# Normalisation roots made by VectorE's Newton step instead of ScalarE, and four w2 loads with a later due time

## The chip, the cores and the metric

The kernel runs on one core of a Trainium2 chip. The metric is the device time of one launch in microseconds; the time before is a median of three runs. A second, profiled execution of the same kernel gives the trace that is read here.

## The reference

One token block of 2048 rows and 1024 columns goes through two sublayers, each behind a modulated layer norm:

```
sa, ca, ga, sb, cb, gb = six rows of silu(c) @ w_mod
h = layernorm(x) * (1 + ca) + sa
x = x + ga * (Cr @ (h @ Dr.T) - Ci @ (h @ Di.T))     # real part of a 2-D DFT
h = layernorm(x) * (1 + cb) + sb
x = x + gb * (gelu(layernorm(h) @ w1 + b1) @ w2 + b2)  # 1024 -> 3584 -> 1024
layernorm(x) = (x - mean) / sqrt(var + 1e-5)
```

So the second half needs two layer norms per row, one on x and one on h, each with its own root.

## The kernel before, in words

All of it happens in the function `fast`. It first normalises the rows (`ln1`, four groups of four row tiles), folds them by the symmetries of the DFT and multiplies by the DFT matrices (`hid_unit`, then `seq_tile` for 16 row tiles, products P and Q, lines 3046 and 3058). The 16 tiles are taken in 8 blocks of two, b = 0 to 7. For each block `ln2` makes both later norms: the sums of squares on ScalarE (line 3120), the scalings on VectorE (lines 3138 to 3162), the final scaling on ScalarE (line 3171). TensorE then transposes the rows (`turn`, line 3181), ScalarE copies them out (line 3185), and `z_tasks` makes seven combinations of them in halves of 16 bits (lines 3211, 3220, 3233), which are written to DRAM for the second half of the rows (line 3226). From about 312 us on the MLP begins: products with w1 (`product3`, line 3628), bias and GELU, products with w2 (line 3742) and the sum over 14 pairs of feature tiles. The matrices are split in seven combinations too (a fast matrix product with seven instead of eight blocks), by the helper lines 2379 (high half, ScalarE), 2391 (low half, VectorE) and 2405 (sums, VectorE).

Each root is made in two steps. `roots` (line 2619) writes on ScalarE r = sqrt(scale * v + bias) (line 2620) and the guarded variance ve = scale * v + bias (line 2621). `newton` (line 2623) improves it on VectorE in four small instructions, lines 2626 to 2629: a = 1 / r, a = a * ve, a = a + r, r = 1 / a. `ln1` calls it on 128x4 values, four times, `ln2` on 128x2 values, twice per block (`root`, lines 3128, 3160 and 3168), which makes 20.

The order of the instructions on each engine is fixed when the program is built. A planner in the kernel keeps a clock per engine and a list of tasks per stream; `pick_first` looks at the first task of every stream in the order of their due times and takes for each engine the first one that can start now, or else the one that starts earliest. A load is a task of the engine "dma" and is issued by SP (SyncE), whose queue is in order: a transfer that waits holds all behind it. Loads share eight semaphores in turn, so a load also waits until the eighth before it has landed.

The loads that matter for the change are issued between 299 and 346 us:

- `early2` (line 3494): four loads of 512 KB, rows of w2 that only serve the squares of its norm (`norm_tasks`, line 3311), which give the scale s2 of the first pair of w2's combinations (`w2_norm`). Due 240, once the products P and Q of tile 15 are done. They go to a place of their own, 144 to 160 KB.
- `raw1` (line 3491): four loads of 256 KB, raw w1 for the groups 3 and 4. Same condition, due 250, to 136 to 144 KB, where operands of product P of the last tiles have lain. Behind them in the same stream stand the four loads `raw2` of w2 (line 3497), due 240, which wait for `turn` 13.
- `w1` (lines 3480 and 3487): the split w1 of the groups 0 to 2, 256 KB each, read back from DRAM, due 200 and 255; they wait for certain turns, the row product of line 2900 or the first products with w1.
- the last block's x (line 3101, 1 MB, due 70), the row of w_mod (line 2894), and the stores of x (line 3148), which are put on SP's queue as soon as the planner has the sum that they store.

Of the kernel before, what the change touches and what calls it, by code (L numbers as in the profile page):

```python
# [12 lines left out]
AF = mybir.ActivationFunctionType  # L13
ALU = mybir.AluOpType
# [3 lines left out]
P = 128  # L18
S = 2048
D = 1024  # L20
# [5 lines left out]
EPS = 1e-5  # L26
# [5 lines left out]
SZ = 256.0  # L32
# [1959 lines left out]
def fast(ctx, tc, x, cre, cim, dre, dim, w1, b1, w2, b2, c, wm, out):  # L1992
# [3 lines left out]
    pe, act, dve, gp, sp = nc.tensor, nc.scalar, nc.vector, nc.gpsimd, nc.sync  # L1996
# [8 lines left out]
    def mk(shape, dt, tag, bufs=1):  # L2005
        cnt[0] += 1
        return pool.tile(shape, dt, tag=tag, name=f"{tag}_{cnt[0]}", bufs=bufs)
# [439 lines left out]
    def add(stream, eng, cost, fn, deps=(), key=None, due=0.0, tag=None):  # L2447
        t = Task(eng, cost, fn, deps, key)
        push(stream, tag or stream, [t], due)
        return t.key  # L2450
# [15 lines left out]
    one, eps4, epsz = (mk([P, 1], F32, n) for n in ("one", "eps4", "epsz"))  # L2466
# [22 lines left out]
    def load(name, f, deps=(), cost=1.4, stream="ld", due=0.0):  # L2489
        return add(stream, "dma", cost, f, deps, name, due)  # L2490
# [125 lines left out]
        nunit[0] += 1  # L2616
        return (nunit[0] - 1) % 3

    def roots(ve, r, v, scale, bias):
        act.activation(r, v, AF.Sqrt, scale=scale, bias=bias[:, 0:1])  # L2620
        act.activation(ve, v, AF.Identity, scale=scale, bias=bias[:, 0:1])

    def newton(ve, r, a):

        return [
            ("dve", 0.17, lambda: dve.reciprocal(a, r)),
            ("dve", 0.17, lambda: dve.tensor_tensor(a, a, ve, op=ALU.mult)),
            ("dve", 0.17, lambda: dve.tensor_tensor(a, a, r, op=ALU.add)),
            ("dve", 0.17, lambda: dve.reciprocal(r, a)),
        ]  # L2630

# [3 lines left out]
    def ln1(bt):  # L2635
        mv, lc = csum[:, 8 * bt : 8 * bt + 8].rearrange("p (q k) -> p q k", k=2), lncs[bt % 2]
        ve, r, a, nm = (lc[:, n] for n in range(4))
        cls, hb = divmod(bt, 2)
        due = 2.0 + 6.0 * bt
        for q in range(4):  # L2640
# [21 lines left out]
            k = add(f"lnq{bt}", "act", 1.35, spread, [("sum", i)], ("spread", i), due)  # L2662
        scale = 0.25 if bt < ACT_STATS else 0.25 / D
        s = [
            ("act", 0.4, lambda: roots(ve, r, mv[:, :, 1], scale, eps4)),
            *newton(ve, r, a),
            ("dve", 0.17, lambda: dve.scalar_tensor_tensor(nm, mv[:, :, 0], -1.0, r, op0=ALU.mult, op1=ALU.mult)),
        ]
        for eng, cost, f in s:
# [183 lines left out]
    for cls in range(2):  # L2853
        f = lambda cls=cls: gp.memset(FA(SPB[cls], (1, 1026), pn=64), 0.0)
# [228 lines left out]
    for n in range(2):  # L3083
        f = lambda n=n: gp.memset(FA(QS[n] + 256, (1, 1)), 0.0)
# [19 lines left out]
    def ln2(b):  # L3104
        y, w, cl = yb(b), wb(b), lns[b % 3]
        su, nm, v, ve, r, a = (cl[:, n, :] for n in range(6))
        due = 78.0 + 22.0 * b
        S_ = f"ln{b % 3}"
        last = [None]

        def step(eng, cost, f, deps=(), key=None):
            last[0] = add(S_, eng, cost, f, [last[0], *deps], key, due)
            return last[0]

        def sq(src, junk, scale, bias, free=None):
            def square(n):
                def f():
                    if free is not None:
                        free(n)
                    act.activation(  # L3120
                        junk[:, n], src[:, n], AF.Square, scale=scale, bias=bias[:, n : n + 1], accum_out=v[:, n : n + 1]
                    )

                return f

            return square

        def root(scale, bias, key=None):
            step("act", 0.4, lambda: roots(ve, r, v, scale, bias), key=key)
            for t in newton(ve, r, a):  # L3130
                step(*t)

        x1 = []
        wfree = w_free(b)
        for n in range(2):
            i = 2 * b + n
            if b in ADDED:
                step("dve", 1.23, lambda n=n: dve.tensor_tensor(y[:, n], y[:, n], ga_t, op=ALU.mult), [("y", i), ("xw", b), *rows])
                k = step("dve", 1.32, lambda n=n: dve.scalar_tensor_tensor(
                    y[:, n], y[:, n], 1.0, w[:, n], op0=ALU.mult, op1=ALU.add, accum_out=su[:, n : n + 1]))  # L3140
            else:
                last[0] = None
                k = step("dve", 1.32, lambda n=n: dve.scalar_tensor_tensor(
                    y[:, n], y[:, n], 1.0, ga_t, op0=ALU.mult, op1=ALU.mult, accum_out=su[:, n : n + 1]), [("y", i), *rows])
                store("xa", i, lambda n=n, i=i: gp.dma_start(y[:, n], x_s[i // 8, i % 8], accum_op=ALU.add), k)
                k = "st", "xa", i
            x1.append(k)
            store("x1", i, lambda n=n, i=i: sp.dma_start(o_s[i // 8, i % 8], y[:, n]), k)
        if b in ADDED:
            step("dve", 0.17, lambda: dve.tensor_scalar(nm, su, -1.0 / D, None, op0=ALU.mult))  # L3150
        else:
            step("dve", 0.17, lambda: dve.scalar_tensor_tensor(
                nm, su, -1.0 / D, csum[:, 4 * b : 4 * b + 4 : 2], op0=ALU.mult, op1=ALU.subtract))
        q = sq(y, w, 1.0, nm)
        for n in range(2):
            step("act", 1.35, q(n), [x1[n], *wfree])
        for n in range(2):
            step("dve", 1.28, lambda n=n: dve.scalar_tensor_tensor(
                w[:, n], y[:, n], nm[:, n : n + 1], cb_t, op0=ALU.add, op1=ALU.mult), key=("sw", 2 * b + n))
        root(0.25 / D, eps4)  # L3160
        for n in range(2):
            step("dve", 1.28, lambda n=n: dve.scalar_tensor_tensor(  # L3162
                w[:, n], w[:, n], r[:, n : n + 1], sb_t, op0=ALU.mult, op1=ALU.add, accum_out=su[:, n : n + 1]))

        q = sq(w, y, -float(D), su, lambda n: reuse("x1", 2 * b + n))
        for n in range(2):
            step("act", 1.35, q(n), key=("ysq", 2 * b + n))
        root(0.25 / (SZ * SZ * D**3), epsz, ("root", b))
        step("dve", 0.17, lambda: dve.scalar_tensor_tensor(nm, su, -1.0 / D, r, op0=ALU.mult, op1=ALU.mult))
        for n in range(2):  # L3170
            f = lambda n=n: act.activation(w[:, n], w[:, n], AF.Identity, scale=r[:, n : n + 1], bias=nm[:, n : n + 1])
            step("act", 1.25, f, key=("w", 2 * b + n))
# [317 lines left out]
    for g, n in ((3, 2), (3, 3), (4, 0), (4, 1)):  # L3490
        f = lambda g=g, n=n: sp.dma_start(raw1(g, n), w1[g, :, PLACE.index(n), :])
        load(("raw1", g, n), f, [("P", 15), ("Q", 15)], 0.75, "rw2", 250.0)
    for q in range(4):
        f = lambda q=q: sp.dma_start(early2(q), w2[0:2, :, q, :].rearrange("j p x -> p j x"))
        load(("early2", q), f, [("P", 15), ("Q", 15)], 1.5, "rw3", 240.0)
    for q in range(4):
        f = lambda q=q: sp.dma_start(raw2(0, q), w2[0:2, :, q, :].rearrange("j p x -> p j x"))
        load(("raw2", 0, q), f, [("turn", 13)], 1.5, "rw2", 240.0)
# [360 lines left out]
    due, t = {}, 0.0  # L3859
# [100 lines left out]
    t = clk["pe"]  # L3960
# [20 lines left out]
    for kind, k in seq:  # L3981
# [17 lines left out]
        else:  # L3999
            v = k  # L4000
# [71 lines left out]
```

## Time and profile before

| what | value |
|---|---|
| median of three runs | 1378.37 us (1377.45 to 1378.69) |
| the profiled execution's own time | 1377.23 us |
| its span | 1375.4 us, mean granted TensorE clock 0.972 |
| PE (TensorE matmul) busy | 1291.3 us, 94% |
| DVE (VectorE) busy | 1088.4 us, 79% |
| ACT (ScalarE) busy | 746.6 us, 54% |
| POOL (GpSimd) busy | 265.1 us, 19% |
| chain that ended last | PE 67%, DVE 9%, ACT 4% of the span |

The span runs from the first to the last instruction of the core. A row of a timeline gives start, duration, engine, line, operation, operands with their shapes, and in brackets how long the engine had been idle before and which instruction let it go on. "SPq" is SP issuing a transfer, not the transfer itself. PEld is TensorE's loading of weights. Line numbers are those of the kernel before.

### The profile page before, as it was taken

To read this page: it belongs to the slowest core of one execution; us is meant where nothing else is said; L and a number is where in the kernel's file an instruction comes from. 1 tells how busy PE (TensorE), PEld (TensorE's weight loads), DVE (VectorE), ACT (ScalarE), POOL (GpSimd) and SP (SyncE) were. 2 spreads that over 40 slices of the span, in tenths; PEclk is the share of its full clock that TensorE was granted. 3 is DMA by queue.
4 is the path that set the end of the run, shared out by engine and by line. 5 is a ranking of instruction groups with operands and counts; after the bars stand their busy time and mean duration, and the time that the engine had idled before them with its cause. 6 is when DMAs were issued, how large, how long until landed. Compare 5 with 4: busy or idle time off the path is not lost.

```text
span 1375.4 us, 17329 instructions
## 1 busy us (share of the span) xinstructions
PE 1291.3 (94%) x6081; PEld 622.9 (45%) x6081; DVE 1088.4 (79%) x1623; ACT 746.6 (54%) x1188; POOL 265.1 (19%) x426
## 2 busy tenths in 40 slices
PE   5888899777989999999999999999999999999997
PEld 1445466543434444444444444444444444444443
DVE  5888789998588999898989996566685858687695
ACT  4476557877667747474746433256545353636330
POOL 2000010102102000000000000254553433553201
PEclk9888899998999999999999999999999999999999
DMA  9777046569536957575453555999797878786524
GB/s 368 307 250 231 1 169 169 133 194 381 218 145 200 320 146 226 171 204 187 153 184 130 200 205 223 262 349 338 252 318 240 296 264 294 268 306 235 176 81 111
DMA packets 109754, 306.22 MB, mean 223 GB/s; under 512 B 14076, under 2 KB 14076, under 8 KB 107736
## 3 DMA queue, kind: packets, MB, share of 16 engines
q1 hardware_dynamic: 76776, 197.73, 40.5%
q0 software_dynamic: 32880, 107.29, 25.9%
q8 instruction: 49, 0.80, 0.2%
q14 instruction: 49, 0.40, 0.1%
HBM read 220.03 MB, written 84.93 MB: 222 GB/s over the span
## 4 chain that ended last, share of the span: by engine, by line
PE 67%; DVE 9%; ACT 4%; issue 2%; DMA 2%; SPq 0%; POOL 0%; DVEq 0%; ACTq 0%; POOLq 0%
PE ps L3742 34%; PE ps L3628 32%; ACT arena L2379 1%; DVE arena L2391 1%; DVE arena L3220 1%; DVE arena L2405 1%; DVE arena L3162 1%; PE ps L3046 1%; DVE arena L3233 1%; DMA arena<-fw 1%; DMA fzc<-arena 1%; ACT arena L3211 1%; DVE arena L3792 0%; DMA arena<-in_w_dram 0%; PE ps L3058 0%
## 5 line engine op out<-in xcount | busy, mean ns | idle before, releaser
L3628 PE MATMUL ps<-arena 128*128 128x512 f16 x2352 | 515.5, 381 | 9.4 <-DMA arena<-fw 4.8
L3742 PE MATMUL ps<-arena 128*128 128x512 f16 x2352 | 513.2, 380 | 8.0 <-ACT arena L3782 6.2
L3628 PEld LDWEIGHTS <-arena 128*128 128x128 f16 x2352 | 230.8, 98 | 289.9 <-issue 10.8
L3742 PEld LDWEIGHTS <-arena 128*128 128x128 f16 x2352 | 230.7, 98 | 288.3 <-issue 12.0
L3792 DVE SCALAR_TENSOR_TENSOR arena<-ps,i4c,arena 128x1024 f32<-128x1024 f32 x179 | 229.5, 1282 | 104.9 <-PE ps L3742 100.4
L2379 ACT ACTIVATE arena<-arena,shc 128x512 f16<-128x512 f32 (+1 forms) x115 | 115.8, 1017 | 137.2 <-DVE arena L2405 80.3
L2391 DVE SCALAR_TENSOR_TENSOR arena<-arena,shc 128x512 f16<-128x512 f32 (+1 forms) x115 | 129.0, 1121 | 29.6 <-ACT arena L2379 29.2
L2405 DVE TENSOR_TENSOR arena<-arena 128x512 f32<-128x512 f32 (+1 forms) x196 | 148.5, 764 | 3.7
L3533 ACT ACTIVATE arena<-arena 128x512 f32<-128x512 f32 (+5 forms) x148 | 91.2, 617 | 108.8 <-DVE arena L3542 84.8
L3647 ACT ACTIVATE arena<-arena,b1s,i1c 128x512 f32<-128x512 f32 x78 | 63.4, 813 | 90.0 <-DVE arena L3654 88.1
L2379 ACT ACTIVATE arena<-arena,s1c 128x512 f16<-128x512 f32 (+1 forms) x70 | 60.9, 886 | 66.5 <-DVE arena L2405 42.2
L3654 DVE TENSOR_TENSOR arena<-arena,ps 128x512 f32<-128x512 f32 x78 | 53.4, 685 | 52.4 <-PE ps L3628 51.7
L3542 DVE TENSOR_TENSOR arena<-arena 128x256 f32<-128x256 f32 x240 | 87.9, 421 | 1.7 <-DMA arena<-in_cre_dram 1.7
L3323 POOL PARTITION_ALL_REDUCE sums<-sums x21 | 10.4, 501 | 405.0 <-DVE sums L3319 405.0
L3559 POOL DMA_DIRECT2D arena<-in_cim_dram x99 | 54.5, 551 | 92.3 <-ACT arena L3533 86.1
L2391 DVE SCALAR_TENSOR_TENSOR arena<-arena,s1c 128x512 f16<-128x512 f32 (+1 forms) x70 | 65.8, 958 | 5.0 <-ACT arena L2379 4.9
L3559 POOL DMA_DIRECT2D arena<-in_cre_dram x99 | 54.6, 552 | 68.3 <-ACT arena L3533 50.9
L3650 ACT ACTIVATE arena<-ps 128x512 f32<-128x512 f32 x78 | 45.8, 588 | 35.8 <-PE ps L3628 35.6
L2391 DVE SCALAR_TENSOR_TENSOR arena<-arena,s2c 128x1024 f16<-128x1024 f32 x49 | 62.0, 1279 | 0.9 <-ACT arena L2379 0.9
L3046 PE MATMUL ps<-arena 128*128 128x256 f16 (+3 forms) x400 | 51.7, 290 | 10.1 <-DVE arena L3073 10.1
L2900 PE MATMUL ps<-arena,scol 128*128 128x512 f32 x128 | 58.3, 602 | 0.3 <-ACT arena L2915 0.3
L2379 ACT ACTIVATE arena<-arena,s2c 128x1024 f16<-128x1024 f32 x49 | 55.0, 1137 | 5.8 <-DVE arena L2405 5.8
(204 smaller groups left out, 1230.7 us busy)
## 6 DMA issues: line engine op xcount, KB each, us to landing
fw<-arena SPq DMA_DIRECT2D x71, 512.0 KB, 5.0
arena<-fw SPq DMA_DIRECT2D x119, 256.0 KB, 4.9
arena<-fw SPq DMA_DIRECT2D x49, 512.0 KB, 7.0
arena<-in_cre_dram POOLq DMA_DIRECT2D x96, 256.0 KB
arena<-in_cim_dram POOLq DMA_DIRECT2D x96, 256.0 KB
arena<-in_wm_dram SPq DMA_DIRECT2D x32, 512.0 KB, 7.5
arena<-in_w_dram SPq DMA_DIRECT2D x32, 512.0 KB, 6.4
arena<-in_w_dram SPq DMA_DIRECT2D x56, 256.0 KB, 4.5
```

What stands on the lines that cost most here:

```text
L2379: act.activation(o[m][0], q(j), AF.Copy, **sc)
L2391: dve.scalar_tensor_tensor(o[m][1], q(j), scale, o[m][0], op0=ALU.mult, op1=ALU.subtract)
L2405: dve.tensor_tensor(q(d), q(a), q(b), op=op)
L2900: pe.matmul(bank((6 if n < 3 else 4) + h), scol[:, k : k + 1].to_broadcast([P, P]), FA(o + 512 * h, (1, 512)), start=k == 0, stop=k == 7,)
L3046: pe.matmul(PA(pb + o, (1, w)), l, r, start=n == 0, stop=n == len(mm_) - 1)
L3533: f = lambda: act.activation(sq(a), sq(a), AF.Square, accum_out=csum[0:pn, n : n + 1])
L3542: dve.tensor_tensor(a[:, o::2], a[:, o::2], b[:, o::2], op=op)
L3559: return lambda t: gp.dma_start(t[0:pn], v)
L3628: pe.matmul(ps.rearrange("p (k t) -> p k t", k=4), w1c[:, m, s, a, d * P : (d + 1) * P], zc(m)[:, b, :, d, :], start=(start and d == 0 and ...
L3647: act.activation(dst, src, AF.Gelu_apprx_tanh, scale=inv, bias=b1s[:, 2 * p + j : 2 * p + j + 1])
L3742: pe.matmul(t[:, j], hidc[:, c_, m, a, k * P : (k + 1) * P], w2c[:, m, c_, w], start=(start and c_ == 0 and n == 0), stop=(c_ == 1 and n = ...
L3792: lambda: dve.scalar_tensor_tensor(dst, ps[b], inv, dst, op0=ALU.mult, op1=ALU.add), kp[b],
```

## The change

`roots` keeps the Sqrt on ScalarE and loses the Identity that wrote ve. `newton` gets the raw variance v, the scale and the guard, and makes the same value in its two middle steps: ve = (v + eps / scale) * a, then a = ve * scale + r. The number of VectorE instructions stays four per root; two TENSOR_TENSOR become two SCALAR_TENSOR_TENSOR with immediate scalars. The planner's cost for the ScalarE step (0.4) and for the VectorE steps (0.17) stays as it was. Besides, the due time of the four `early2` loads goes from 240 to 300.

```diff
-    def roots(ve, r, v, scale, bias):
+    def roots(r, v, scale, bias):
         act.activation(r, v, AF.Sqrt, scale=scale, bias=bias[:, 0:1])
-        act.activation(ve, v, AF.Identity, scale=scale, bias=bias[:, 0:1])
-
-    def newton(ve, r, a):
+
+    def newton(ve, r, a, v, scale, eps):
 
         return [
             ("dve", 0.17, lambda: dve.reciprocal(a, r)),
-            ("dve", 0.17, lambda: dve.tensor_tensor(a, a, ve, op=ALU.mult)),
-            ("dve", 0.17, lambda: dve.tensor_tensor(a, a, r, op=ALU.add)),
+            ("dve", 0.17, lambda: dve.scalar_tensor_tensor(ve, v, eps / scale, a, op0=ALU.add, op1=ALU.mult)),
+            ("dve", 0.17, lambda: dve.scalar_tensor_tensor(a, ve, scale, r, op0=ALU.mult, op1=ALU.add)),
             ("dve", 0.17, lambda: dve.reciprocal(r, a)),
         ]
...
-            ("act", 0.4, lambda: roots(ve, r, mv[:, :, 1], scale, eps4)),
-            *newton(ve, r, a),
+            ("act", 0.4, lambda: roots(r, mv[:, :, 1], scale, eps4)),
+            *newton(ve, r, a, mv[:, :, 1], scale, EPS / 4),
...
-        def root(scale, bias, key=None):
-            step("act", 0.4, lambda: roots(ve, r, v, scale, bias), key=key)
-            for t in newton(ve, r, a):
+        def root(scale, bias, eps, key=None):
+            step("act", 0.4, lambda: roots(r, v, scale, bias), key=key)
+            for t in newton(ve, r, a, v, scale, eps):
                 step(*t)
...
-        root(0.25 / D, eps4)
+        root(0.25 / D, eps4, EPS / 4)
...
-        root(0.25 / (SZ * SZ * D**3), epsz, ("root", b))
+        root(0.25 / (SZ * SZ * D**3), epsz, EPS / (4 * SZ * SZ), ("root", b))
...
         f = lambda q=q: sp.dma_start(early2(q), w2[0:2, :, q, :].rearrange("j p x -> p j x"))
-        load(("early2", q), f, [("P", 15), ("Q", 15)], 1.5, "rw3", 240.0)
+        load(("early2", q), f, [("P", 15), ("Q", 15)], 1.5, "rw3", 300.0)
```

## The prediction, made before the result was known

> **What bounds the kernel now.** I read first the span and clock, then the chain that ended last, then the busy time by stage.
>
> ```profile
> core 0: 1375.4 us, clock 0.972
> 476.38 36.26 PE ps L3742 x168
> ...
> 1274.09 36.26 PE ps L3742 x168
> 205.00:250.00 45.00, 37.37 (x252) 24.98 (x250) 41.05 (x79) 35.96 (x58) 4.38 (x6) 0.95 0.58 153
> 250.00:300.00 50.00, 42.95 (x276) 28.70 (x275) 46.98 (x82) 38.27 (x59) 4.29 (x5) 0.91 0.58 149
> 300.00:342.00 42.00, 30.33 (x111) 14.81 (x110) 37.66 (x65) 33.53 (x50) 11.42 (x16) 0.87 1.01 360
> 342.00:405.00 63.00, 55.88 (x258) 25.72 (x257) 45.10 (x65) 43.56 (x58) 6.21 (x9) 0.96 0.50 187
> ```
>
> The profiled execution took 1377.23 us, its span 1375.4 us, so 1.8 us lie around the span; the median of the three timed runs is 1378.37 us, 1.1 us above the profiled execution. From 476 us to 1310 us the chain is TensorE alone, one block of 168 matmuls in 36.26 us after another, so nothing that the change touches can be worth anything there. All that can be won or lost lies before 476 us. In the stage rows the columns are length, then busy time of PE, PEld, DVE, ACT and POOL, the clock, the DMA share and GB/s. Between 205 and 300 us VectorE is busy 88 of 95 us, ScalarE 74; from 300 to 342 us the DMA engines are full (1.01) and VectorE still has 37.66 of 42 us. So the second layer norm is bound by VectorE with ScalarE close behind, and its end, with the loads of w1 for the first products, by VectorE and DMA together.
>
> **The left-out ScalarE instruction.**
>
> ```profile
> L2621 ACT ACTIVATE lns<-lns,eps x8: 279/283/291, 208.9 to 346.8; 128x2 f32<-128x2 f32 x8
> L2621 ACT ACTIVATE lns<-lns,epsz x8: 279/279/280, 213.9 to 354.2; 128x2 f32<-128x2 f32 x8
> L2621 ACT ACTIVATE lnc<-csum,eps x4: 280/281/282, 12.0 to 85.4; 128x4 f32<-128x4 f32 x4
> 208.74 0.29 ACT L2620 ACTIVATE lns<-lns,eps 128x2 f32<-128x2 f32 x1
> 208.93 0.28 ACT L2621 ACTIVATE lns<-lns,eps 128x2 f32<-128x2 f32 x1
> 209.06 0.17 DVE L2626 RECIPROCAL lns<-lns 128x2 f32<-128x2 f32 x1 [0.64 <-ACT lns L2620]
> 209.33 0.16 DVE L2627 TENSOR_TENSOR lns<-lns 128x2 f32<-128x2 f32 x1
> 209.53 0.16 DVE L2628 TENSOR_TENSOR lns<-lns 128x2 f32<-128x2 f32 x1
> 209.72 0.17 DVE L2629 RECIPROCAL lns<-lns 128x2 f32<-128x2 f32 x1
> 306.17 0.16 DVE L3169 SCALAR_TENSOR_TENSOR lns<-lns 128x2 f32<-128x2 f32 x1
> L2627 DVEq EVENT_SEMAPHORE  x20: 21/21/21, 12.3 to 354.6; - x20
> ```
>
> Twenty Identity instructions go, sixteen of them in the second layer norm. Each holds ScalarE for about 0.2 us (start to start, 208.74 to 208.93), though it lasts 0.28. But the reciprocal starts behind the Sqrt, not behind the Identity: the Identity runs beside the reciprocal. So only what stands behind it on ScalarE can gain 0.2 us.
>
> VectorE keeps four instructions per root. Two TENSOR_TENSOR of 128x2 (0.16 us) become two SCALAR_TENSOR_TENSOR of 128x2, which a neighbouring line shows at 0.16 us as well: nothing for the operations. What goes is a wait: L2627 has a semaphore instruction of its own, and its start lies 0.27 us behind that of the reciprocal, where the next steps follow in 0.20 and 0.19. The new first product reads the raw sum of squares, which ScalarE wrote before the Sqrt that VectorE has already waited for, so no wait takes its place. That is 0.07 us a root at most, 0.05 where the reciprocal is the shorter one; I take 0.06.
>
> ```profile
> 209.33 0.17 DVE lns L2627
> ...
> 326.56 0.17 DVE lns L2627
> ```
>
> Of these steps 12 stand on the chain that ended last, the first at 209.33 and the last at 326.56: 12 x 0.06 = 0.7 us. The bounds are 0 (the wait stays in another form) and 12 x 0.2 = 2.4 us (ScalarE's share carried through at each); I stay at 0.7, because on the chain the roots are rows of VectorE and of the Sqrt, and the Identity isn't among them. The four roots of the first layer norm lie before the part that the chain view reaches, between 0 and 4 x 0.2 = 0.8 us; I take 0, since no view puts them on the chain.
>
> **The moved loads.** The four loads at L3494 are 512 KB each (as the code has them) and are at present first in their group on SP's queue; the four of L3491 (raw w1, 256 KB each, due 250) come behind.
>
> ```profile
> 295.04 5.30 PE L3046 MATMUL ps<-arena 128*128 128x257 f16 x24 [3.15 <-DVE arena L3073]
> 299.51 0.39 SPq L3494 DMA_DIRECT2D arena<-in_w_dram  x1
> 301.43 0.39 SPq L3101 DMA_DIRECT2D arena<-in_x_dram  x1
> 301.87 1.91 SPq L3494 DMA_DIRECT2D arena<-in_w_dram  x3
> 303.83 1.59 SPq L3491 DMA_DIRECT2D arena<-in_w_dram  x2
> 311.61 0.98 SPq L3491 DMA_DIRECT2D arena<-in_w_dram  x2
> DMA  0000996999999999999999999999999899999999
> ```
>
> With due 300 the planner takes the four L3491 loads first; then, until the turns and products that the other reloads wait for are done, its queue has nothing else ready, so I expect three L3494 loads around 302 to 305 and the fourth at 311.6, behind the store that SP holds there. By bytes: before the store four of L3494, two of L3491 and the 1 MB of L3101 went out, 3.5 MB; now three, four and that, 3.5 MB again; behind it 0.5 MB either way. The last row is the DMA share from 295 to 345 us in steps of 1.25 us: full from 303.75 on. The same bytes in the same full queue ahead of the w1 reloads cost nothing. The one new wait: the first L3491 load overwrites operands of the product at 295.04, whose end is 300.34, while the L3494 load could start at 299.51. Behind it on SP stands L3101, which goes at 301.43 either way. Price between 0 and 0.8 us; I take 0, for the byte count.
>
> The squares of these rows are four ScalarE instructions of the norm that gives w2's scale.
>
> ```profile
> L3311 ACT ACTIVATE arena<-arena x4: 1037/1052/1057, 308.6 to 322.4; 128x1024 f16<-128x1024 f32 x4
> 323.48 1.13 ACT L3120 ACTIVATE arena<-arena,lns 128x1024 f32<-128x1024 f32 x1
> 331.62 1.06 ACT L3211 ACTIVATE arena<-arena 128x1024 f16<-128x1024 f32 x1 [0.94 <-DVE arena L3233]
> 371.06 2.18 ACT L2379 ACTIVATE arena<-arena,s2c 128x1024 f16<-128x1024 f32 x2
> ```
>
> The first, now at 308.6, has no data in time and goes to the others, which end right before 323.48; the last will find its place near 331, where ScalarE waits 0.94 us. It is 1.05 us long against those 0.94, so some tenths spill over, into the 4.3 us that VectorE has idle between 300 and 342 us. The scale itself is read at 371.06, some 35 us later. I take 0 here, ends 0 and 1.2 us (one whole square in front of L3120).
>
> **What the end does with it.**
>
> ```profile
> 332.44 4.29 SPq L3480 DMA_DIRECT2D arena<-fw  x4
> 336.93 1.09 PE L3181 MATMUL ps<-ident,arena 128*128 128x128 f32 x8 [2.03 <-ACT arena L3185]
> 341.75 8.62 PE L3628 MATMUL ps<-arena 128*128 128x512 f16 x32 [3.73 <-DMA arena<-fw]
> 404.50 7.70 PE L3742 MATMUL ps<-arena 128*128 128x512 f16 x23 [6.21 <-ACT arena L3782]
> 310.76:314.18 3.42, 2.14 (x6) 0.50 1.04 404
> 341.48:344.90 3.42, 3.15 (x8) 0.50 1.03 413
> 402.92:406.34 3.42, 1.84 (x5) 0.50 0.83 334
> ```
>
> The reloads at 332.44 stand on SP behind a store that waits for VectorE, so a shorter VectorE chain moves them and with them the restart of TensorE at 341.75. The sum: 1378.37 - 0.7 + 0 + 0 = 1377.7 us (1376.5 for the profiled execution).
>
> After a pause TensorE runs at half clock (0.50 in the last three rows: length, PE busy, clock, DMA). The clock came back to full behind the stretch that was busy 3.15 of 3.42 us, not behind those with 2.14 and 1.84; so where a restart falls in such a stretch is worth up to 1.2 us: a restart 1 us earlier might spare the second half-speed stretch. The Trainium skill ("TensorE: Matmul & The Clock Gate", Part 1) says that the clock is judged in free-running windows of about 3.4 us. The trace agrees in the length, 3.42 us; by that rule an earlier restart at 341.75 stays slow until the same 344.90 and keeps only half of the 0.7, which makes 1378.0; by the row alone it keeps all, and the sum goes by that.
>
> **The rivals.** *Relief of the queue (faster).* If due 300 puts the L3494 loads behind the w1 reloads (due 200 and 255), 2.1 MB leave the full queue ahead of the load for 341.75. At 413 GB/s that is 5.1 us; TensorE's own transposes (336.93 + 1.09) end at 338.0, so 3.7 are usable, of which the half-speed stretch takes some 0.7: 1378.4 - 0.7 - 3.0 = 1374.7 us. For it: restart waits for DMA. Against: SP's queue has pauses, 305 to 311, in which loads that are ready will be sent.
>
> *Clock stretches move (faster).* If ScalarE's 0.2 us carry through at some roots, the restart in 310.76 to 314.18 comes 1 us earlier, and so does that at 404.50; both return to full clock a stretch earlier, 2 x 1.2 us, beside about 1 us of shift: 1378.4 - 3.4 = 1375.0 us. For it: 2.14 and 1.84 of 3.42 us are near the middle. Against: 0.7 us is below the 1 us that is needed.
>
> *A late restart (slower).* All four squares stand before 323.48 (+1.2), the first load waits (+0.8), and the w1 reloads slip by the 1.3 us that are left beside Newton's 0.7. Then the stretch from 341.48 is busy 1.9 of 3.42 us, as in the two rows that stayed slow, and TensorE runs at half clock 3.4 us longer: +1.7. The restart at 404.50 adds some 0.3. In all +3.3: 1381.7 us. It decides once the restart is over about 0.3 us late. For it: only 0.27 us of that stretch are free now. Against: VectorE, not ScalarE, is last before 326.
>
> *The change does nothing:* the semaphore wait stays and bytes are bytes: 1378.4 us.
>
> **How the numbers follow.** Forecast 1377.7 (0.32), nothing 1378.4 (0.02), relief 1374.7 (0.22), clock stretches 1375.0 (0.19), late restart 1381.7 (0.25). A measurement of this kernel tells about 0.2%, 2.8 us, from no change; so faster has 0.22 + 0.19 = 0.41, same 0.34, slower 0.25. The forecast's own range is 1376.0 (2.4 for the roots) to 1379.2 (0.8 for the load). With cases of both signs the range has to reach both: from 1372.8 (relief, and a clock stretch spared with its shift, 1374.7 - 1.2 - 0.7) to 1381.8 (just over the late restart); what lies outside are larger sums of the same, under 0.2.
>
> **What would show it.** L2621 has no ScalarE row, L2627 no semaphore row, and the product starts 0.20 us behind the reciprocal. In SP's rows L3491 stands before L3494, with three of the latter before 311 and one behind. TensorE restarts near 341.0, 341.75 - 0.7; a time near 338 means relief, one behind 342.0 the late restart. If the granted clock is 1.00 right behind 314.18 or 406.34, the stretches moved. I am wrong at the root if the stage from 342 to 405 us changes its length by over 1 us, since I expect its order of work unchanged.

## The result, and the profile after

The changed kernel takes 1370.15 us (median of 7 runs, 1366.74 to 1372.83) where the kernel before, beside it, takes 1377.45 us (7 runs, 1374.38 to 1378.69). The ratio is 0.9949, 95% interval 0.9932 to 0.9967: about 7 us faster, outside the range that was given. A second set of runs of the changed kernel gave 0.9951 (0.9935 to 0.9968).

First the span and clock of the kernel after, its stages, and from its chain of waits the pieces around 475 us; then the stage from 405 us of the kernel before, which had not been shown.

```profile
core 0: 1368.4 us, clock 0.973
300.00:342.00 42.00, 30.61 (x97) 14.05 (x96) 35.47 (x57) 30.83 (x45) 8.05 (x12) 0.84 0.96 350
342.00:405.00 63.00, 60.62 (x292) 28.67 (x291) 50.76 (x77) 47.79 (x61) 9.06 (x16) 1.00 0.57 208
405.00:475.00 70.00, 67.24 (x312) 30.29 (x311) 58.77 (x87) 50.62 (x66) 11.00 (x16) 1.00 0.79 223
473.10 1.21 DVE arena L3791
474.35 31.25 PE ps L3741 x144
505.61 36.26 PE ps L3627 x168
```

```profile
405.00:475.00 70.00, 68.68 (x307) 30.42 (x306) 59.51 (x90) 49.76 (x65) 11.73 (x16) 0.97 0.80 241
```

In both profiled executions the first transposes start at 217.35 us, so their times compare directly. Up to 342 us nothing is won. From 342 to 405 us TensorE is busy 60.62 us instead of 55.88 us, at clock 1.00 instead of 0.96. From 505 us on it is bound by TensorE as before, 36.26 us for 168 matmuls. So the gain is made between 342 and 475 us. The timeline of TensorE after says where:

```profile
322.47 4.26 PE L3627 MATMUL ps<-arena 128*128 128x512 f16 x12 [2.79 <-DMA arena<-fw]
341.56 2.76 PE L3627 MATMUL ps<-arena 128*128 128x512 f16 x12 [1.37 <-DMA arena<-fw]
393.29 5.34 PE L3741 MATMUL ps<-arena 128*128 128x512 f16 x24
398.92 13.32 PE L3741 MATMUL ps<-arena 128*128 128x512 f16 x61 [0.29 <-ACT arena L3781]
474.35 6.00 PE L3741 MATMUL ps<-arena 128*128 128x512 f16 x27 [2.76 <-DVE arena L3791]
```

The first two products with w2 start at 393.29 us, 0.3 us later than before (392.95). The third follows after 0.29 us of idle time instead of 6.21 us: 398.92 instead of 404.50 us. It runs at full clock, where before it crossed a half-speed stretch; by the fifth product the lead is 8.2 us, and 10.0 us at 466.25 us, two short waits of before, 0.70 and 0.62 us, being gone as well. A new wait of 2.76 us at 474.35 us takes 2.9 us back; 7.0 us remain to the end (1368.4 against 1375.4). A pause costs twice when the clock is low behind it: 6.21 us idle was followed by clock 0.50, 2.76 us idle by 1.00. The Trainium skill ("TensorE: Matmul & The Clock Gate", "Why this matters for your kernels") advises against gaps above about 3 us for that reason; these two rows agree. The length alone does not decide, though: the pause of 2.79 us ahead of 322.47 us in the same trace was followed by clock 0.50, and its 12 matmuls took 4.26 us.

The third product waits for ScalarE's copy of the first. The rows of ScalarE, before and then after:

```profile
356.94 1.23 ACT L3171 ACTIVATE arena<-arena,lns 128x1024 f32<-128x1024 f32 x1
359.02 1.23 ACT L3171 ACTIVATE arena<-arena,lns 128x1024 f32<-128x1024 f32 x1
360.25 1.28 ACT L3924 ACT_TABLE_LOAD   x1
369.12 1.13 ACT L2379 ACTIVATE arena<-arena,shc 128x1024 f16<-128x1024 f32 x1
389.13 0.72 ACT L2379 ACTIVATE arena<-arena,s1c 128x512 f16<-128x512 f32 x1 [2.39 <-DVE s1c L3340]
390.37 0.71 ACT L2379 ACTIVATE arena<-arena,s1c 128x512 f16<-128x512 f32 x1
403.36 1.09 ACT L3782 ACTIVATE arena<-ps,i4c 128x1024 f32<-128x1024 f32 x1
```

```profile
349.76 1.28 ACT L3923 ACT_TABLE_LOAD   x1
351.90 1.24 ACT L3170 ACTIVATE arena<-arena,lns 128x1024 f32<-128x1024 f32 x1
354.00 1.23 ACT L3170 ACTIVATE arena<-arena,lns 128x1024 f32<-128x1024 f32 x1
361.18 1.14 ACT L2379 ACTIVATE arena<-arena,shc 128x1024 f16<-128x1024 f32 x1
397.77 1.10 ACT L3781 ACTIVATE arena<-ps,i4c 128x1024 f32<-128x1024 f32 x1
398.76 1.33 ACT L2379 ACTIVATE arena<-arena,s1c 128x512 f16<-128x512 f32 x2
```

Two things have changed places. The first GELU, whose table load shows in the trace, stood behind the last block's two scalings (L3171) and stands ahead of them (L3170): 349.76 instead of 360.25 us, so the hidden tiles' splitting (operand shc) starts at 361.18 instead of 369.12 us. And the splitting of w1's group 3 (operand s1c) stood ahead of the copy (operand i4c) and stands behind it. Neither is in the diff. On VectorE it is one of the sums of the first products with w1 that changed places with the last block's root, here first before, then after:

```profile
348.74 0.69 DVE L3933 TENSOR_TENSOR arena<-arena,ps 128x512 f32<-128x512 f32 x1 [6.29 <-PE ps L3628]
349.35 0.16 DVE L2626 RECIPROCAL lns<-lns 128x2 f32<-128x2 f32 x1
```

```profile
344.86 0.16 DVE L2625 RECIPROCAL lns<-lns 128x2 f32<-128x2 f32 x1
349.19 0.68 DVE L3932 TENSOR_TENSOR arena<-arena,ps 128x512 f32<-128x512 f32 x1
```

The planner made these choices. Apart from the left-out Identity, the two orders first differ on ScalarE at the square of 308.65 us, on VectorE at 309.36 us and on TensorE at the transposes of 336.93 us (times of the kernel before). By the planner's rule (first in due order that can start now) a square that leaves that gap changes what fits into every later one. The runs below show that the due time alone brings the new order; that it does so by way of the squares is read from the rule and from this first difference, and no run moved the squares alone.

### The profile page after: what moved, and what is told of

Its sections match the earlier page's. It is cut to its first block, busy times and chain, and to the rows that moved or that the text cites. A ratio compares the mean times of both kernels' runs of the same rounds, so it can differ in the third digit from the quotient of the medians.

```text
span 1368.4 us, 17290 instructions
## 1 busy us (share of the span) xinstructions
PE 1290.4 (94%) x6081; PEld 624.5 (46%) x6081; DVE 1089.3 (80%) x1623; ACT 744.6 (54%) x1168; POOL 264.2 (19%) x426
## 4 chain that ended last, share of the span: by engine, by line
PE 66%; DVE 10%; ACT 3%; DMA 2%; issue 2%; POOL 0%; SPq 0%; DVEq 0%; ACTq 0%; POOLq 0%
PE ps L3741 34%; PE ps L3627 31%; DVE arena L2391 2%; DVE arena L3219 1%; DVE arena L3161 1%; ACT arena L2379 1%; DVE arena L2405 1%; PE ps L3045 1%; DMA arena<-fw 1%; DVE arena L3232 1%; PE ps L3057 1%; DVE arena L3791 1%; DMA frow_gbb<-arena 0%; DVE arena L3653 0%; DMA arena<-in_w_dram 0%
## 5 line engine op out<-in xcount | busy, mean ns | idle before, releaser
L3532 ACT ACTIVATE arena<-arena 128x512 f32<-128x512 f32 (+5 forms) x148 | 91.2, 617 | 108.5 <-DVE arena L3541 89.7
L3558 POOL DMA_DIRECT2D arena<-in_cim_dram x99 | 54.5, 550 | 92.3 <-ACT arena L3532 89.3
L3310 ACT ACTIVATE ps<-arena 128x1024 f32<-128x1024 f32 x46 | 46.7, 1016 | 19.2 <-DMA arena<-in_w_dram 9.0
```

The costliest lines, as they stand in the source:

```text
L3532: f = lambda: act.activation(sq(a), sq(a), AF.Square, accum_out=csum[0:pn, n : n + 1])
L3558: return lambda t: gp.dma_start(t[0:pn], v)
```

## The experiments

A ratio is to the kernel before on the same chip, with its 95% interval. "Copy stretch" is the time from the first to the third product with w2 in the profiled execution (before 11.55, after 5.63 us). The other columns are times behind the start of the first transposes, since that start itself lies between 212.6 and 217.7 us in different executions.

| version | median us | ratio | GELU table load | copy stretch | third w2 product | end |
|---|---|---|---|---|---|---|
| before | 1374.8 to 1377.5 | 1 | 142.9 | 11.55 | 187.2 | 1158.0 |
| after | 1370.15 | 0.9949 [0.9932, 0.9967] | 132.4 | 5.63 | 181.6 | 1151.0 |
| after, again | 1368.08 | 0.9951 [0.9935, 0.9968] | 135.0 | 5.63 | 184.5 | 1153.9 |
| new roots only | 1373.72 | 0.9987 [0.9970, 1.0004] | 142.5 | 11.56 | 186.8 | 1158.0 |
| due 300 only | 1371.96 | 0.9980 [0.9965, 0.9995] | 134.2 | 5.62 | 183.1 | 1152.7 |
| after, loads in old order | 1369.51 | 0.9965 [0.9948, 0.9981] | 134.2 | 5.64 | 183.5 | 1152.9 |
| before, loads in new order | 1376.09 | 0.9999 [0.9984, 1.0014] | 141.5 | 11.55 | 185.8 | 1156.8 |
| before, pause filled | 1373.56 | 0.9990 [0.9974, 1.0006] | 142.5 | 11.56 | 186.8 | 1157.2 |
| last norm due 205 | 1365.20 | 0.9920 [0.9902, 0.9939] | 130.4 | 5.18 | 178.6 | 1147.9 |
| after, last norm due 242 | 1366.90 | 0.9953 [0.9933, 0.9973] | 133.8 | 5.42 | 180.6 | 1151.6 |
| sum behind | 1369.87 | 0.9958 [0.9942, 0.9974] | 134.7 | 5.18 | 181.9 | 1151.1 |
| root behind | 1374.85 | 0.9993 [0.9981, 1.0005] | 144.0 | 11.12 | 188.0 | 1160.1 |
| sum moved | 1377.72 | 1.0012 [0.9997, 1.0026] | 143.0 | 11.55 | 187.3 | 1158.8 |
| sum back | 1371.66 | 0.9970 [0.9954, 0.9986] | 136.7 | 5.18 | 185.0 | 1154.6 |
| GELU behind | 1377.87 | 1.0013 [1.0001, 1.0025] | 140.1 | 11.12 | 189.2 | 1160.6 |
| GELU ahead | 1375.40 | 1.0002 [0.9991, 1.0013] | 137.9 | 6.26 | 181.8 | 1157.4 |
| w1 group 3 late | 1375.12 | 0.9995 [0.9982, 1.0008] | 140.9 | 9.21 | 182.8 | 1155.6 |
| w1 group 3, all late | 1373.30 | 0.9987 [0.9972, 1.0002] | 143.0 | 9.22 | 185.0 | 1158.8 |
| new roots, last norm due 205 | 1362.59 | 0.9912 [0.9892, 0.9932] | 130.2 | 5.18 | 177.5 | 1146.7 |

One profiled execution says less than these columns suggest. "After", "after, again", "due 300 only" and "after, loads in old order" run one and the same order of instructions on TensorE, VectorE, ScalarE and GpSimd (but for the roots' own instructions). Their copy stretch is 5.62 to 5.64 us each time, but their third product lies anywhere from 181.6 to 184.5 us and their end from 1151.0 to 1153.9 us. "Before", "new roots only" and "before, loads in new order" share the other order, with 11.55 to 11.56, 185.8 to 187.2 and 1156.8 to 1158.0 us. So the profiles bear out a gain of 3 to 7 us at the end, of which the pair shown above has the most, and a difference of under 3 us in the last two columns is not shown by one execution.

**The change in parts.** New roots with due 240, and the old roots with due 300.

> The new Newton step with the loads of w2's rows still due 240, so every engine keeps the order of work of the kernel before. If the gain is the changed order (first theory), this is worth 0 to -1 us against before, and the third product with w2 starts near 404, as before. If the ScalarE time that the left-out instruction frees is what counts (second theory), at least half of the 7 us are here and that product starts before 401.

> Only the due time goes to 300; the roots are made as before. The first theory (changed order) expects -6 to -7.5 us against before and the third product with w2 near 399, since the planner's order is that of the changed kernel. The second theory (freed ScalarE time) expects less than half of it, -3 us at most.

> The changed kernel itself, on the same chip as the next three, as their measure: 5 to 7.5 us below the kernel before.

The new roots alone keep every instruction's place: TensorE's restart (341.75 us before) comes 1.0 us earlier behind the first transposes (123.4 instead of 124.4 us), the third product with w2 0.4 us, the end 0.1 us. Due 300 alone has the changed kernel's order and its copy stretch of 5.62 us. So the order comes from the due time. By the ratios the parts are 1.8 and 2.8 us, together 4.6 us; the changed kernel with its loads in the old order gains 4.8 us on the same chip, and the changed kernel itself 6.7 us on another. The 2.8 us (interval 0.7 to 4.8) miss the 6 to 7.5 that the first theory expected; by the time alone the second theory would allow them. What speaks for the order is the copy stretch, and against freed ScalarE time that the new roots alone start the third product at 403.41 us, not before 401. No run here splits the gain more finely.

**Is it the transfers?** Both kernels once more with SP issuing the eight loads in the other's sequence, all tasks staying where they are (a table gives each load's place in the planner another load to issue).

```diff
-        load(("early2", q), f, [("P", 15), ("Q", 15)], 1.5, "rw3", 300.0)
+        load(("early2", q), issue(E_(q)), [("P", 15), ("Q", 15)], 1.5, "rw3", 300.0)
```

> The changed kernel, but its eight loads of raw w1 and of w2's rows are issued by SP in the sequence of the kernel before; the order of work on the computing engines stays that of the changed kernel. If the order of the computing engines carries the gain, the time stays within 1.5 us of the changed kernel's (1370). If the transfers' order or their share of the DMA queue carries it (third theory), 3 us or more of the 7 are lost.

> The kernel before, but SP issues its eight loads of raw w1 and w2's rows in the changed kernel's sequence; the computing engines keep the order of before, with one square of w2 early on ScalarE. First theory: no gain, 0 to +3 us, since that square now waits for its data. If the transfers' sequence carries the gain: -3 us or better.

The sequence of the transfers shows no gain by itself (0.9999, interval 0.9984 to 1.0014). Without it the changed kernel keeps 4.8 us (0.9965). Its median is within 1.5 us of 1370, as expected for the order; by the ratio it gains 2.2 us less than the changed kernel in its first runs, with intervals that overlap. So most of the gain comes with the planner's order, and not with the sequence of the transfers.

**Is it the half-speed stretch?** The kernel before with the second product issued twice, to keep TensorE busy in the pause (it then counts twice in the sum).

```diff
+                if v == 0 and blk == 0 and m == 1:
+                    part(blk, m, ps[b], (0, 1))
```

> The kernel before, with the second product with w2 (12 matmuls) issued twice, so that TensorE works some 2.6 us in its pause ahead of the third product at 404.5; all else as before, the result the same. If the half-speed stretch behind that pause is worth what the milestones show (7.76 us between the third and the fifth product before, 5.17 after), the stretch goes and the time falls by 2 to 2.6 us. If that stretch lies beside other work that is as late, the time stays within 0.7 us.

```profile
401.85 10.46 PE L3742 MATMUL ps<-arena 128*128 128x512 f16 x35 [3.62 <-ACT arena L3784]
```

0.9990, with an interval that holds 1; the 1.4 us lie between the two cases. But the run does not answer the question. The row of the third product shows that 3.62 us of the pause are left, and the first 13 matmuls behind it still run at clock 0.50 (401.85 to 407.10 us). What the half-speed stretch is worth stays open; "GELU ahead" below has no slow matmul behind its third product, and no gain.

**An earlier last norm.** My first theory was that the last block's norm (due 232) comes earlier in the changed kernel, and that this pays.

```diff
-        due = 78.0 + 22.0 * b
+        due = 78.0 + 22.0 * b if b < 7 else 205.0
```

> The kernel before, old roots, loads due 240; only the last block's norm gets due 205 instead of 232, which puts its first additions on VectorE's queue ahead of block 6's scalings, as in the changed kernel. If the gain is that this norm, and with it the splitting of w2, is done earlier, this gives 4 us or more of it, and the third product with w2 starts 4 us or more earlier than before. If the squares' or loads' new place is what counts, under 1.5 us.

> The changed kernel, new roots, loads due 300; only the last block's norm gets due 242 instead of 232. Its first additions come later (planner's order), the squares and loads stay late. First theory: 4 us or more of the gain are lost, the time is within 2.5 us of the kernel before. Rival (squares and loads): the gain stays, within 1.5 us of the changed kernel.

Due 205 in the kernel before gives 0.9920, better than the change (the intervals just overlap). But the changed kernel with due 242 keeps its gain (0.9953). An earlier norm is enough and not needed; the theory in that form falls.

**The sum at the head of VectorE's queue.** Its replacement was the 6.29 us in which VectorE waits for TensorE in front of the last block's root. Two runs change the sum's place and let the planner plan on; a third tries the splitting of w1's group 3.

```diff
# sum behind (on before); ("sb", i) is a new key of the scalings L3162
-  f, [k, ("g3e", g, n)], ("g3s", g, n), 215.0, "g3")]
+  f, [k, ("g3e", g, n), *([("sb", 15)] if (g, n) == (0, 3) else [])], ("g3s", g, n), 215.0, "g3")]
# root behind (on after)
-                step(*t)
+                step(*t, [("g3s", 0, 3)] if b == 7 and key is None else [])
# w1 group 3 late (on before): push_w1(3) moved from ahead of the loop to the end of gemm3(2)
```

> The kernel before, but VectorE's sum of the first products with w1 (L3933) may only stand behind the last block's scalings (L3162). Loads, squares, roots and all of VectorE's order up to 342 us stay those of before. Theory A (a sum at the head of VectorE's queue, waiting 6.3 us for TensorE's first products with w1 while the last block's root is ready behind it, is where the changed kernel wins): the idle 6.3 us in front of the root goes, the stretch from the first to the third product with w2 shortens from 11.55 us to 5 to 7 us, time ratio 0.993 to 0.997 (about 1369 us). Theory C (what wins is that the last block's two additions and the store behind them come 11 us earlier in the planner's order): stretch 11.5 us and ratio 0.999 to 1.001, since those stay where they are.

> The changed kernel, but the last block's first root may only stand behind VectorE's sum of the first products with w1, as it does in the kernel before. Roots, loads, squares and the early additions of the last block stay those of the changed kernel. Theory A: an idle time of 3 to 6 us is back in front of the root, the stretch from the first to the third product with w2 is 10.5 to 12 us again, ratio to before 0.998 to 1.000 (what is left is Newton's 0.7 to 1 us). Theory C: stretch 5.6 us and ratio 0.995 as in the changed kernel.

> The kernel before, but the splitting of w1's group 3 is handed to the planner only ahead of the products with w2, which puts its three VectorE pieces (1.9 us) behind ScalarE's copy of the first product. Theory B (the changed kernel wins because these pieces no longer stand ahead of that copy): stretch from the first to the third product with w2 near 5.6 us, ratio 0.995. Theory A (they only move because the idle time ahead is filled): the 6.3 us idle in front of the root stays, the stretch shortens by no more than the pieces, to 9.5 to 11.5 us, ratio 0.998 to 1.001.

In stretch and time the first two came out as theory A had it: one place in the queue gives 0.9958 on the kernel before and takes the changed kernel back to 0.9993. But the idle time that should be back in "root behind", 3 to 6 us, is only 0.66 us. The third run speaks against B, but missed A's numbers: the stretch is 9.21 us, just under A's 9.5, and the idle time in front of the sum is 0.93 us, not 6.3, at the same total time. So the wait itself could hardly be the price. Nor is the root ready for all of it, as theory A says. Rows of ScalarE before:

```profile
346.08 0.60 ACT L3928 ACTIVATE arena<-ps 128x512 f32<-128x512 f32 x1 [4.95 <-PE ps L3628]
346.58 0.29 ACT L2620 ACTIVATE lns<-lns,eps 128x2 f32<-128x2 f32 x1
```

The root's Sqrt (L2620) stands on ScalarE behind a copy that itself waits 4.95 us for TensorE, and starts only 2.8 us before the reciprocal of 349.35 us. (That place does not decide either: in "sum behind" the Sqrt still stands behind such a copy, in "root behind" ahead of it.) The next two move only that place and leave all other instructions where they are: the sum behind the scalings in the order of before, and the root behind the sum in the order of "sum behind".

```diff
# sum moved (on before): the planner's task issues nothing, the last scaling issues it
+            if (g, n) == (0, 3):
+                kept_back.append(f)
+                f = lambda: None
...
+                if (b, n) == (7, 1):
+                    kept_back.pop()()
```

> The kernel before with one single instruction elsewhere: VectorE's sum L3933 that stands ahead of the last block's root is issued behind the block's two scalings (L3162); every other instruction of every engine keeps the order of before. If the wait at the head of VectorE's queue is itself the price: the stretch from the first to the third product with w2 falls from 11.55 to 6 to 8.5 us, ratio 0.995 to 0.997. If the price is the order that the planner chooses behind it (tile 15's transposes later on TensorE, the splitting of w1's group 3 ahead of the copy): stretch 10 to 11.5 us, ratio 0.998 to 1.000.

> The earlier run that had the sum behind the scalings (ratio 0.9958), with the root's four steps and the scalings issued behind the sum again; all else keeps that run's order. If the wait itself is the price: stretch from the first to the third product with w2 9 to 11.5 us, ratio 0.998 to 1.000. If the order behind it is: stretch 5 to 6.5 us, ratio 0.995 to 0.997.

The two rows are of "sum moved": VectorE's root, and the third product on TensorE (here L3749).

```profile
347.02 0.17 DVE L2626 RECIPROCAL lns<-lns 128x2 f32<-128x2 f32 x1 [4.56 <-ACT lns L2620]
404.62 7.67 PE L3749 MATMUL ps<-arena 128*128 128x512 f16 x23 [6.21 <-ACT arena L3789]
```

The root comes 2.3 us earlier, all that the Sqrt allows, and the pause on TensorE is 6.21 us as before: 1.0012. Stretch and ratio lie just above what was expected for the order as the price, and far from theory A. With a wait put back (2.60 us in front of the sum) and the faster order kept, the stretch stays at 5.18 us and the ratio is 0.9970. Against the 0.9958 without it the wait is worth 1.7 us by the ratios, whose intervals overlap; in the two profiles the third product comes 3.0 us and the end 3.5 us later. So the wait is not what the copy stretch follows, and theory A falls as the main price, though a part of the time may be the wait's. The sum matters mainly because of the order that is planned behind it.

**GELU and w1's group 3.** All the faster versions have a table load before 137 us (in the table) and VectorE's pieces of the splitting of w1's group 3 behind the copy; none of the slower ones has both. ScalarE's two pieces need not be behind it: in "last norm due 205", "sum behind", "sum back" and "new roots, last norm due 205" they stand right ahead of the copy, and TensorE has no pause.

```diff
# GELU behind (on after)
-  f, [*deps, ("root", NB - 1)], ("quad", g, n), 266.0)
+  f, [*deps, ("root", NB - 1), *([("w", 15)] if g == 0 else [])], ("quad", g, n), 266.0)
# GELU ahead (on before)
-            step("act", 1.25, f, key=("w", 2 * b + n))
+            step("act", 1.25, f, [("quad", 0, PLACE[0])] if b == 7 else [], key=("w", 2 * b + n))
# w1 group 3, all late (on before): pushed behind the copy of the first product with w2
+                    if (v, blk, m) == (0, 0, 0):
+                        push_w1(3)
+                        push_w1(4)
```

> The changed kernel, but ScalarE's GELU of the first w1 products (with the table load before it) may only stand behind the last block's two scalings on ScalarE (L3170), as it stands in the kernel before; in the changed kernel the first GELU stands ahead of them. Roots, loads, squares, the block's additions and VectorE's sum keep their places. If this place decides: first table load 8 to 11 us later, stretch from the first to the third product with w2 10.5 to 12 us, ratio to before 0.998 to 1.000. If not: 5.6 us and 0.995.

> The kernel before, but the last block's two scalings on ScalarE (L3171) may only stand behind one GELU of the first w1 products; nothing else is constrained. If this place decides: the splitting of the first hidden tiles starts 4 us or more earlier, the stretch from the first to the third product with w2 is 5 to 7.5 us, ratio 0.995 to 0.998. If not: 11.5 us, 0.999 to 1.001.

> The kernel before with all of the splitting of w1's group 3 (two ScalarE and three VectorE pieces) handed to the planner only once ScalarE's copy of the first product with w2 is issued. If these pieces ahead of the copy are the whole price: stretch 5 to 6 us, ratio 0.995. If they are only its smaller part, and the later start of GELU and of the hidden tiles' splitting the rest: stretch 7.5 to 9.5 us, ratio 0.997 to 1.000.

Rows of ScalarE and TensorE, first of "GELU behind", then of "GELU ahead" (third product, and a later one with w1):

```profile
355.62 1.22 ACT L3170 ACTIVATE arena<-arena,lns 128x1024 f32<-128x1024 f32 x1
356.85 1.28 ACT L3923 ACT_TABLE_LOAD   x1
405.94 6.38 PE L3741 MATMUL ps<-arena 128*128 128x512 f16 x21 [5.78 <-ACT arena L3781]
```

```profile
398.84 5.34 PE L3742 MATMUL ps<-arena 128*128 128x512 f16 x24 [0.92 <-ACT arena L3782]
438.22 23.61 PE L3628 MATMUL ps<-arena 128*128 128x512 f16 x108 [2.03 <-ACT arena L3650]
467.68 7.03 PE L3628 MATMUL ps<-arena 128*128 128x512 f16 x24 [1.98 <-ACT arena L3650]
```

With the GELU behind the scalings the changed kernel loses everything (1.0013): counted from the first transposes the table load is 7.7 us later, just under the 8 to 11 expected; the planner puts w1's group 3 ahead of the copy again and the pause is back at 5.78 us. The ratio is just above the 0.998 to 1.000 expected. With one GELU ahead, the kernel before has its third product 5.3 us earlier and a stretch of 6.26 us, as expected (the hidden tiles' splitting only 2.5 us earlier, not 4); but it gives that back in waits for ScalarE such as those at 438.22 and 467.68 us, and the time is 1.0002, not the 0.995 to 0.998 expected. Taking all pieces of w1's group 3 out from ahead of the copy shortens the stretch by 2.3 us (9.22 us, within what was expected); the time is 0.9987, with an interval that holds 1.

VectorE's time from the transposes of tile 8 (counted from 0) to the third product with w2 splits the 5.6 us in two. Before it is 91.2 us busy and 22.5 idle; after 89.1 and 19.0; with w1's group 3 all late 89.3 and 22.3. So 2.1 us are work that no longer stands ahead of the copy, and 3.5 us are idle time that is gone, most likely since hidden tiles can be split earlier. In "last norm due 205" it is 92.2 and 12.8: there the idle time alone makes the gain. In other executions of the order after, the idle time is 20.6 to 21.9 us, so the second part varies with the execution.

**The version that the runs point to.** The new roots with due 240, and the last norm due 205:

> The version that the runs point to: new roots, the four loads' due time left at 240, the last block's norm due 205 instead of 232. The planner's order is that of the earlier run with the last block due 205 alone (1365.2 us, ratio 0.992). If Newton's saving adds to it: 1364.3 us, ratio 0.991; if what it saves is waited for elsewhere: 1365.2 us, ratio 0.992.

1362.59 us, 0.9912: the fastest here, and better than both kernels. Its interval (0.9892 to 0.9932) overlaps that without the new roots (0.9902 to 0.9939), so that the roots add to it isn't shown by the times; in the profiles the third product comes 1.1 us and the end 1.2 us earlier, less than executions of one kernel differ.

## Why the prediction was wrong, point by point

**The roots: right as far as TensorE's restart.** Rows of VectorE after:

```profile
209.19 0.17 DVE L2625 RECIPROCAL lns<-lns 128x2 f32<-128x2 f32 x1 [0.51 <-ACT lns L2620]
209.39 0.16 DVE L2626 SCALAR_TENSOR_TENSOR lns<-lns 128x2 f32<-128x2 f32 x1
209.58 0.16 DVE L2627 SCALAR_TENSOR_TENSOR lns<-lns 128x2 f32<-128x2 f32 x1
```

The product starts 0.20 us behind the reciprocal (it was 0.27), and no new wait takes the place of the old. The step of 0.7 us measured 1.0 us at TensorE's restart and 0.1 us at the end of "new roots only"; by the times 1.8 us with an interval of -0.6 to 4.1. The size was fair as far as the roots reach (with old roots and the same order, the restart lies at 123.6 to 124.6 us in three executions, against 123.4). Where the rest went shows at the restart, first in "new roots only", then before:

```profile
340.01 17.89 PE L3627 MATMUL ps<-arena 128*128 128x512 f16 x72 [3.00 <-DMA arena<-fw]
341.75 17.25 PE L3628 MATMUL ps<-arena 128*128 128x512 f16 x72 [3.73 <-DMA arena<-fw]
```

The same 72 matmuls take 0.64 us longer, because ten of them instead of seven run at half clock; 0.4 us of the 1.0 are left behind them, and the third product keeps that. The prediction had weighed this loss of about half, and then let its sum go "by the row alone", in which all is kept. In these two executions the other reckoning was the right one.

**The order of the loads: right.** SP's rows after:

```profile
299.56 1.21 SPq L3490 DMA_DIRECT2D arena<-in_w_dram  x2
300.88 0.40 SPq L3100 DMA_DIRECT2D arena<-in_x_dram  x1
301.33 1.06 SPq L3490 DMA_DIRECT2D arena<-in_w_dram  x2
302.43 2.12 SPq L3493 DMA_DIRECT2D arena<-in_w_dram  x3
310.40 0.36 SPq L3147 DMA_DIRECT2D out_dram<-arena  x1
310.81 0.49 SPq L3493 DMA_DIRECT2D arena<-in_w_dram  x1
```

Raw w1 first, three loads of w2 by 304.6 us and the fourth behind the store, as forecast. The first did not wait: it goes at 299.56 us. No run shows another price than 0 for them (0.9999, which is good to about 2 us).

**The squares, and the order behind them: the step that failed.** "I take 0 here" followed them through ScalarE as the old order has it, and the prediction said of the stage from 342 to 405 us "I expect its order of work unchanged". In the trace after the squares run later than was thought there, from 319.65 to 339.60 us, but the scale still comes in time for its first reader:

```profile
319.65 1.05 ACT L3310 ACTIVATE arena<-arena 128x1024 f16<-128x1024 f32 x1
...
338.56 1.04 ACT L3310 ACTIVATE arena<-arena 128x1024 f16<-128x1024 f32 x1
...
369.55 1.14 ACT L2379 ACTIVATE arena<-arena,s2c 128x1024 f16<-128x1024 f32 x1
```

So no delay by way of the scale shows, as said. But the order is planned anew from the first of them on: the last block's root ahead of the sum, the GELU ahead of the scalings, w1's group 3 behind the copy. The copy stretch is 5.9 us shorter for it in every execution of this order. In the pair of profiles shown above that is 5.6 us at the third product, and 8.2 us at the fifth, with the half-speed stretch. The prediction put this at nothing: its sum holds only what each moved piece costs by itself. It had named the sign of its failure (the length of that stage by over 1 us), and had no rival for it.

**The rivals.** The relief of the queue did not happen: w2's loads went ahead of w1's reloads, and TensorE restarted at 341.56, not near 338 us. A late restart did not happen in this profile either; but in the other three executions of the same order TensorE restarts 1.5 to 2.4 us later behind the first transposes than before ("after, again" at 344.02 us), and the shorter copy stretch more than makes up for it. Clock stretches did move, but with the new order and not as that rival had it: the one at 404.50 us is gone with the shorter pause, the one at 341.75 us is gone, and a new one stands at 322.47 us. The restart in front of 314 us is still at half clock. Weighing the Trainium skill's free-running windows ("TensorE: Matmul & The Clock Gate", Part 1) at the restart of 341.75 us had no effect in the kernel after: TensorE paused only 1.37 us there and ran its 12 matmuls in 2.76 us, at full clock.

**What stays open.** Why some versions keep the earlier third product to the end ("sum behind" 5.2 us there and 7.0 at the end, after 5.6 and 7.0) and others give it back by 475 us ("GELU ahead" 5.3 and 0.6, "w1 group 3 late" 4.4 and 2.4) was not isolated; with one profile of each, only the 0.6 against 7.0 is clear. Which place in the new order carries the time stays open as well: two single constraints take the changed kernel back to the time of before, but each lets the planner choose anew behind it. Nor was a gain for the new roots that is outside their own interval.

## What to carry to other kernels

Where a planner fixes the order when the program is built, a changed due time or a moved task is first of all another order, and its price lies where the plans part, often far behind the edit: compare the two orders of instructions on every engine before pricing any of the moved work. A long wait at the head of a queue need not be what costs; look whether what stands behind it is ready, and test it by moving that one instruction alone before building on it. And an earlier milestone is only a gain if the later ones come earlier too, so follow it to the stage that is bound by one engine.

## What the runs showed that I had not expected

The first transposes start anywhere from 212.62 to 217.73 us in the profiled executions, whatever the kernel (after 217.35 and 217.19, "sum behind" 213.08), and the runs of the kernel before on one chip spread from 1369.72 to 1379.34 us. That is as much as the effect measured here, so a difference of 0.2% needs many runs, and milestones are best counted from a point behind the first stage. Even so counted, the changed kernel's own two profiles differ by 2.9 us at the third product, so one execution of each is not enough for a milestone.
